# A fused attention and gated feed-forward block: side work moved to other places beside the matmul stream, with another DMA order and other buffer counts

## The chip, the core and the metric

The kernel runs on one core of a Trainium2 chip. The metric is the device time of one execution in microseconds (us); the median of three runs before the change is 272.18 us (271.14 to 272.46). The engines are named as the profile names them: PE (TensorE matmuls), PEld (its weight loads), DVE (VectorE), ACT (ScalarE), POOL (GpSimd) and SP (SyncE, which issues every DMA of this kernel). Each engine works through its own instructions in the order in which the program was written; between engines there are semaphores.

## What is computed

```python
x = A_x                                  # 1 x 2048 x 512, bf16
xn = layernorm(x)
qkv = xn @ wqkv                          # 512 x 1536; 32 heads of 16
# each position attends to 8 positions: itself and 2, 4, ... 14 positions back
logits = einsum("bhsd,bhswd->bhsw", q, kg) * 16 ** -0.5    # masked where idx < 0
o = einsum("bhsw,bhswd->bhsd", softmax(logits), vg)
s = o.reshape(B, S, D) @ wo              # 512 x 512
h = gelu(xn @ w_gate) * (xn @ w_up)      # 512 x 1792, twice
g = silu(h @ w_down)                     # 1792 x 512
return x + s * g
```

## The kernel before, in words

The 2048 positions are cut into four blocks of 512 (index j), and each block into four tiles of 128 (index t over all 16). Nothing reorders the program: the schedule is manual, so the order of the Python calls is the order on each engine. Per block, PE runs three long stages, and they are the frame for everything else:

- `qkv(j, 0..11)`: twelve groups of four 128x512 matmuls. Four give `q_sb`, four give `k_sb`, and four give V, which ACT copies into a staging tile `vst` and SP stores to `vT` in DRAM (L216).
- `glu(j, 0..13)`: fourteen pairs of four matmuls (`g_ps`, `u_ps`), ACT makes `ge` (Gelu) and `u`, DVE multiplies them into `h`.
- `down(j, 0..3)`: for each tile fourteen matmuls `y_ps` and four `s_ps`; ACT makes `sl` (Silu), DVE computes `m` and `o_t`, and SP stores `o_t` (L357).

Stages run as qkv 0, glu 0, qkv 1, down 0, glu 1, qkv 2, down 1, glu 2, qkv 3, down 2, glu 3, down 3. Beside them stands the side work:

- The layer norm of tile t: `moments(t)` (DVE `stats`, `mv`, then two POOL instructions for `rstd`), `normalize(t)` (DVE `xn`) and a transpose on PE (four small matmuls into the one PSUM tile `tr`, L179), copied by ACT into `xnT`.
- The window attention of block j: eight products `pk` (DVE, L235, 128x2048 each), summed over the head dimension on PE by `logits(j, 0)` and `logits(j, 1)` (`L_ps`), exponentiated on ACT (`E`), summed by `denominators` (`den_ps`, DVE reciprocal `rs`), spread over partitions (`sp_ps`, ACT `rb`), multiplied with V in eight products `pv` (DVE, L293) and summed on PE by `av_sum` (`o_ps`, then DVE `oT`). `pk` and `pv` share eight slots (`prod`), and `L_ps`, `den_ps`, `sp_ps` and `o_ps` share two PSUM banks (`att`).
- `load_v(j)` reads the shifted V windows back from `vT`, in four DMAs of 520 KB (L222). It needs all four `vst` stores of its block.

In the kernel before, `normalize(t)` transposes at once. Tiles 4 to 7 are normalized within qkv 0; tiles 8 to 11 have their moments ahead of, and their normalization behind, each tile of down 0; tiles 12 to 15 have both within qkv 2. `load_v(j + 1)` stands in one piece ahead of down j. `vst` has 3 buffers and `o_t` 2. SP issues x, wqkv, the gate and up weights, then w_down (`wd`), the rest of x and wo, and only then the small DMA of zeros into `vT` (`zpad`) and the first `vst` stores.

Of the kernel before, what the change touches and what calls it, by code (L numbers as in the profile page):

```python
# [28 lines left out]
def kernel(  # L29
# [23 lines left out]
    def pool(name, bufs, **kw):  # L53
        return ctx.enter_context(tc.tile_pool(name=name, bufs=bufs, **kw))
# [40 lines left out]
    for i in range(3):  # L95
        load_w(wqkv_sb, A_wqkv, i * D, (i + 1) * D)
    load_x(TPQ, TPQ)
    for lo, hi in ((0, DF // 2), (DF // 2, DF)):
        load_w(wg_sb, B_w_gate, lo, hi)
        load_w(wu_sb, B_w_up, lo, hi)  # L100
    nc.sync.dma_start(out=wd_sb[:], in_=B_w_down.rearrange("(k p) n -> p k n", p=P))
    load_x(2 * TPQ, TPQ)
    load_x(3 * TPQ, TPQ)
    for g in range(NC):
        nc.sync.dma_start(  # L105
            out=wo_sb[:, g, :],
            in_=bass.AP(tensor=A_wo.tensor, offset=g * 4 * D, ap=[[D, 4], [DH * D, H], [1, D]]),
        )


    ident = const.tile([P, P], BF16, name="ident")
# [21 lines left out]
        band(dsum[:, c, 8 * c : 8 * c + 8], 0, 16, 16, 1, 8)  # L133

    hsum = const.tile([P, H], BF16, name="hsum")
    for j in range(WL):
        nc.vector.tensor_copy(
            out=hsum[H * j : H * (j + 1), :], in_=ident[H * j : H * (j + 1), H * j : H * (j + 1)]
        )

    spread = const.tile([P, 4, P], BF16, name="spread")
    nc.vector.memset(spread[:], 0.0)
    for q in range(4):
        for j in range(4):
            nc.vector.tensor_copy(
                out=spread[H * q : H * (q + 1), q, H * j : H * (j + 1)],
                in_=ident[H * q : H * (q + 1), H * q : H * (q + 1)],
            )

    xnT = {}  # L150
    k_sb = big.tile([P, NC, PAD + S], BF16, name="k_sb")
# [8 lines left out]
    def moments(t):  # L160
# [4 lines left out]
        )  # L165
        nc.gpsimd.tensor_tensor(out=rstd[:, t, :], in0=rstd[:, t, :], in1=mhalf[:], op=ALU.pow)

    def normalize(t):
        xn = sm2.tile([P, D], BF16, name="xn")
        nc.vector.tensor_scalar(  # L170
            out=xn[:], in0=x_sb[:, t, :], scalar1=mv[:, t, 0:1], scalar2=rstd[:, t, :],
            op0=ALU.subtract, op1=ALU.mult,
        )
        transpose(t, xn)

    def transpose(t, xn):
        tr = trp.tile([P, NC * P], BF16, name="tr")
        for c in range(NC):
            nc.tensor.transpose(tr[:, c * P : (c + 1) * P], xn[:, c * P : (c + 1) * P], ident[:])  # L179
# [21 lines left out]
    def qkv(j, fo):  # L201
# [5 lines left out]
        if which == 0:  # L207
            nc.scalar.activation(out=st[j]["q"][:, c, :], in_=ps[:], func=AF.Copy)  # L208
        elif which == 1:
            lo = PAD + j * TQ  # L210
            nc.scalar.activation(out=k_sb[:, c, lo : lo + TQ], in_=ps[:], func=AF.Copy)  # L211
        else:
            vst = sm.tile([P, TQ], BF16, name="vst")
            nc.scalar.activation(out=vst[:], in_=ps[:], func=AF.Copy)  # L214
            lo = PAD + j * TQ
            nc.sync.dma_start(out=vT[c * P : (c + 1) * P, lo : lo + TQ], in_=vst[:])  # L216

    def load_v(j):

        va = vap.tile([P, DH, VW], BF16, name="v_arr")  # L220
        for wl in range(WL):
            nc.sync.dma_start(  # L222
                out=va[H * wl : H * (wl + 1), :, :],
                in_=bass.AP(
# [2 lines left out]
                    ap=[[SV * DH, H], [SV, DH], [1, VW]],  # L227
                ),
            )
        st[j]["va"] = va  # L230

    def qk_product(j, w):
        pk = prod.tile([P, NC, TQ], BF16, name="pk", tag="prod")
# [97 lines left out]
    def down(j, tt):  # L331
# [24 lines left out]
        nc.vector.tensor_tensor(out=o_t[:], in0=m[:], in1=x_sb[:, t, :], op=ALU.add)  # L356
        nc.sync.dma_start(out=out2d[t * P : (t + 1) * P, :], in_=o_t[:])  # L357


    for t in range(TPQ):  # L360
        moments(t)
        if t:
            normalize(t - 1)
    normalize(TPQ - 1)
    for t in range(TPQ, 2 * TPQ):
        moments(t)
    for fo in range(3 * NC):
        qkv(0, fo)
        if fo in (2, 4, 6, 8):
            normalize(TPQ + fo // 2 - 1)  # L370
    load_v(0)
    for j in range(NJ):
        for fc in range(NF):
            if j == 0:
                if fc < W:
                    qk_product(j, fc)
                if fc == 5:
                    logits(j, 0)
                if fc == 9:
                    logits(j, 1)  # L380
# [48 lines left out]

# [1 line left out]
_INS = ['A_x', 'A_wqkv', 'A_wo', 'B_x', 'B_w_gate', 'B_w_up', 'B_w_down']  # L431
_OUTS = [((1, 2048, 512), 'bfloat16')]
# [25 lines left out]
```

## Time and profile before

| What | us |
|---|---|
| Median of three runs | 272.18 |
| The profiled execution, its own time | 271.04 |
| Its span, first to last instruction | 269.3 |
| PE busy | 235.2 |
| DVE busy | 148.3 |
| ACT busy | 146.8 |
| POOL busy | 16.2 |

PE is busy for 87% of the span, and the next engine for 55%. The chain that ended last is PE for 71% of the span. The profiled execution's time is 1.74 us above its span. A window of the trace is given as its start and end in us from the span's start; in it, the busy time of an engine is followed by its count of instructions.

### The profile page before, as it was taken

What the parts mean: (1) busy time and instruction counts of PE and PEld (TensorE: products, weight loads), DVE (VectorE), ACT (ScalarE), POOL (GpSimd) and SP (SyncE); (2) the same over time, 40 slices, a digit from 0 to 9 for tenths busy, and PEclk for the clock granted to TensorE, in tenths of its full rate; (3) what the DMA queues carried; (4) which work ended last, traced back from release to release, by engine and by line L of the source; (5) the groups of instructions that cost most, each with busy time, mean ns of one, the idle gap of its engine ahead of it and who ended that gap; (6) DMA issues with size and microseconds to landing.
All of it is one profiled execution on the core that took longest, in us unless ns stands there. A gap on an engine that the chain in (4) does not pass through costs nothing.

```text
span 269.3 us, 3429 instructions
## 1 busy us (share of the span) xinstructions
PE 235.2 (87%) x1296; PEld 100.3 (37%) x1296; DVE 148.3 (55%) x242; ACT 146.8 (55%) x226; POOL 16.2 (6%) x60
## 2 busy tenths in 40 slices
PE   0599149999996769999899989999999959999993
PEld 0354013444332324434344434334444414334441
DVE  7631019537877671985454764893036454893231
ACT  1375057996551618665675638656773337656410
POOL 5430000000011110000130000000000000000000
PEclk9999858999999999999999999999999979999999
DMA  6999619600029700000004950000025920000001
GB/s 195 364 380 351 194 44 210 104 4 0 0 79 209 149 19 19 2 0 0 2 19 128 199 111 19 0 2 0 0 80 115 200 80 3 0 0 1 8 33 39
DMA packets 21793, 22.66 MB, mean 84 GB/s; under 512 B 1552, under 2 KB 21776, under 8 KB 21776
## 3 DMA queue, kind: packets, MB, share of 16 engines
q1 hardware_dynamic: 21776, 22.43, 32.6%
q8 instruction: 10, 0.16, 0.3%
q14 instruction: 7, 0.06, 0.1%
HBM read 18.22 MB, written 4.21 MB: 83 GB/s over the span
## 4 chain that ended last, share of the span: by engine, by line
PE 71%; SPq 11%; DMA 9%; DVE 6%; issue 1%; ACT 0%; POOL 0%; DVEq 0%; ACTq 0%
PE g_ps L191 19%; PE u_ps L191 18%; PE y_ps L334 12%; PE qkv_ps L191 11%; DMA out_dram<-o_t 7%; SPq L83 4%; PE s_ps L345 4%; PE o_ps L305 3%; PE L_ps L244 3%; SPq L89 3%; SPq L105 2%; DMA vT<-vst 2%; DVE m L354 2%; DVE pk L235 2%; DVE o_t L356 1%
## 5 line engine op out<-in xcount | busy, mean ns | idle before, releaser
L191 PE MATMUL g_ps<-xnT,wg_sb 128*128 128x512 bf16 x224 | 59.7, 390 | 9.0 <-ACT vst L214 9.0
L191 PE MATMUL u_ps<-xnT,wu_sb 128*128 128x512 bf16 x224 | 58.3, 383 | 0.0
L328 DVE TENSOR_TENSOR h<-ge,u 128x512 bf16<-128x512 bf16 x56 | 23.7, 423 | 59.7 <-ACT u L326 59.6
L334 PE MATMUL y_ps<-wd_sb,h 128*128 128x512 bf16 x224 | 51.0, 379 | 0.0
L191 PE MATMUL qkv_ps<-xnT,wqkv_sb 128*128 128x512 bf16 x192 | 45.2, 387 | 0.7 <-ACT xnT L183 0.7
L235 DVE TENSOR_TENSOR pk<-q_sb,k_sb 128x2048 bf16<-128x2048 bf16 x32 | 38.0, 1219 | 9.4 <-ACT k_sb L211 9.4
L324 ACT ACTIVATE ge<-g_ps 128x512 bf16<-128x512 f32 x56 | 33.6, 599 | 16.7 <-PE g_ps L191 16.6
L326 ACT ACTIVATE u<-u_ps 128x512 bf16<-128x512 f32 x56 | 33.5, 598 | 14.0 <-PE u_ps L191 14.0
L293 DVE TENSOR_TENSOR pv<-E,v_arr 128x2048 bf16<-128x2048 bf16 x32 | 38.6, 1217 | 0.0
L191 PEld LDWEIGHTS <-wg_sb 128*128 128x128 bf16 x224 | 20.5, 100 | 39.0 <-issue 19.1
L191 PEld LDWEIGHTS <-wu_sb 128*128 128x128 bf16 x224 | 22.1, 99 | 27.5 <-issue 1.8
L334 PEld LDWEIGHTS <-h 128*128 128x128 bf16 x224 | 21.5, 98 | 26.3 <-issue 1.3
L342 ACT ACTIVATE sl<-y_ps 128x512 bf16<-128x512 f32 x16 | 9.6, 597 | 33.2 <-PE y_ps L334 33.2
L354 DVE TENSOR_TENSOR m<-s_ps,sl 128x512 bf16<-128x512 f32 x16 | 11.1, 691 | 29.7 <-PE s_ps L345 29.7
L191 PEld LDWEIGHTS <-wqkv_sb 128*128 128x128 bf16 x192 | 18.5, 100 | 22.8 <-issue 3.8
L179 PE MATMUL tr<-ident,xn 128*128 128x128 bf16 x64 | 7.0, 240 | 16.2 <-DVE xn L170 14.2
L214 ACT ACTIVATE vst<-qkv_ps 128x512 bf16<-128x512 f32 x16 | 9.6, 597 | 17.4 <-DMA vT<-vst 12.0
L183 ACT ACTIVATE xnT<-tr 128x512 bf16<-128x512 bf16 x16 | 9.5, 595 | 17.2 <-PE tr L179 17.2
L345 PE MATMUL s_ps<-wo_sb,oT 128*128 128x512 bf16 x64 | 16.4, 379 | 0.0
L244 PE MATMUL L_ps<-pk,dsum 128*32 128x512 bf16 x128 | 10.9, 406 | 4.0 <-DVE pk L235 4.0
L208 ACT ACTIVATE q_sb<-qkv_ps 128x512 bf16<-128x512 f32 x16 | 9.6, 597 | 6.6 <-PE qkv_ps L191 6.6
L179 PEld LDWEIGHTS <-xn 128*128 128x128 bf16 x64 | 4.9, 105 | 20.8 <-DVE xn L170 18.7
(40 smaller groups left out, 133.0 us busy)
## 6 DMA issues: line engine op xcount, KB each, us to landing
v_arr<-vT SPq DMA_DIRECT2D x16, 520.0 KB, 10.2
vT<-vst SPq DMA_DIRECT2D x16, 128.0 KB, 1.7
out_dram<-o_t SPq DMA_DIRECT2D x16, 128.0 KB, 3.5
wg_sb<-in_B_w_gate_dram SPq DMA_DIRECT2D x2, 896.0 KB
wu_sb<-in_B_w_up_dram SPq DMA_DIRECT2D x2, 896.0 KB, 12.3
wd_sb<-in_B_w_down_dram SPq DMA_DIRECT2D x1, 1792.0 KB, 16.7
wqkv_sb<-in_A_wqkv_dram SPq DMA_DIRECT2D x3, 512.0 KB, 5.3
x_sb<-in_A_x_dram SPq DMA_DIRECT2D x3, 512.0 KB, 13.4
```

The source lines that it names most:

```text
L83: nc.sync.dma_start(out=x_sb[:, t : t + n, :], in_=x2d[t * P : (t + n) * P, :].rearrange("(t p) d -> p t d", p=P),)
L179: nc.tensor.transpose(tr[:, c * P : (c + 1) * P], xn[:, c * P : (c + 1) * P], ident[:])
L191: nc.tensor.matmul(ps[:], lhsT=w[:, dk, lo : lo + P], rhs=xnT[j][:, dk, :], start=(dk == 0), stop=(dk == NC - 1),)
L235: nc.vector.tensor_tensor(out=pk[:], in0=st[j]["q"][:], in1=k_sb[:, :, off : off + TQ], op=ALU.mult)
L244: nc.tensor.matmul(L[H * wl : H * (wl + 1), :], lhsT=dsum[:, c, :], rhs=st[j]["pk"][WL * wh + wl][:, c, :], start=(c == 0), stop=(c == NC ...
L293: nc.vector.tensor_tensor(out=pv[:], in0=st[j]["E"][:, wh, :].unsqueeze(1).to_broadcast([P, 4, TQ]), in1=st[j]["va"][:, 4 * g : 4 * g + 4, ...
L324: nc.scalar.activation(out=ge[:], in_=g_ps[:], func=AF.Gelu_apprx_tanh)
L326: nc.scalar.activation(out=u[:], in_=u_ps[:], func=AF.Copy)
L328: nc.vector.tensor_tensor(out=h[:], in0=ge[:], in1=u[:], op=ALU.mult)
L334: nc.tensor.matmul(y[:], lhsT=st[j][fc][:, tt * P : (tt + 1) * P], rhs=wd_sb[:, fc, :], start=(fc == 0), stop=(fc == NF - 1),)
L345: nc.tensor.matmul(s[:], lhsT=st[j]["oT"][:, g, tt * P : (tt + 1) * P], rhs=wo_sb[:, g, :], start=(g == 0), stop=(g == NC - 1),)
L354: nc.vector.tensor_tensor(out=m[:], in0=s[:], in1=sl[:], op=ALU.mult)
```

## The change

The calls of the side work move into a table (`at`), keyed by stage, block and position, and `run` calls what the table holds ahead of each PE group. The mathematics, the tiles and the instructions' shapes are as they were. The parts are:

1. DMA order on SP: the last two pieces of x go behind each half of the gate and up weights; `wd` and `wo` are issued after qkv 0 and `load_v(0)`.
2. `vst`, `o_t` and `xn` come from a pool of 4 buffers (3, 2 and 2 before); `q_sb`, `rb` and `oT` have 1 buffer (2 before).
3. The copies that build `hsum` and `spread` on DVE move from the program's start behind the normalization of the first four tiles.
4. `normalize` no longer transposes. The moments of tiles 8 to 11 go into qkv 0, their normalization into glu 0, their transposes into qkv 1; the moments of tiles 12 to 15 go into glu 0, their normalization and transposes into qkv 2.
5. Block 0's attention: `logits(0, 0)` at glu position 6 (5 before), `logits(0, 1)` at 10 (9), `denominators` at 12 (11), the spread and six `pv` products in qkv 1; each `av_sum` one position later there, its products apart from it.
6. Blocks 1 to 3: `logits(j, 0)` ahead of the last tile of down j-1 (the third before), `logits(j, 1)` at glu position 1 (0), `denominators` at 2 (1), the spread at 4 (3), each `av_sum` at 6, 8, 10, 12 (5, 7, 9, 11); three of the eight `pk` products of blocks 2 and 3 at the end of their qkv stage.
7. `load_v(j)` for j of 1 to 3 is cut into its four DMAs, one ahead of each tile of down j-1.

```diff
-    qp = pool("qp", 2)
+    qp = pool("qp", 1)
-    op = pool("op", 2)
+    op = pool("op", 1)
+    sm4 = pool("sm4", 4)
...
-    for lo, hi in ((0, DF // 2), (DF // 2, DF)):
+    for i, (lo, hi) in enumerate(((0, DF // 2), (DF // 2, DF))):
         load_w(wg_sb, B_w_gate, lo, hi)
         load_w(wu_sb, B_w_up, lo, hi)
-    nc.sync.dma_start(out=wd_sb[:], in_=B_w_down.rearrange("(k p) n -> p k n", p=P))
-    load_x(2 * TPQ, TPQ)
-    load_x(3 * TPQ, TPQ)
-    for g in range(NC):
-        nc.sync.dma_start(
-            out=wo_sb[:, g, :],
...
+        load_x((2 + i) * TPQ, TPQ)
+
+    def load_late_weights():
+        nc.sync.dma_start(out=wd_sb[:], in_=B_w_down.rearrange("(k p) n -> p k n", p=P))
...
     def normalize(t):
-        xn = sm2.tile([P, D], BF16, name="xn")
+        xn = xns[t] = sm4.tile([P, D], BF16, name="xn")
...
-        transpose(t, xn)
...
-            vst = sm.tile([P, TQ], BF16, name="vst")
+            vst = sm4.tile([P, TQ], BF16, name="vst")
...
-        o_t = sm2.tile([P, D], BF16, name="o_t")
+        o_t = sm4.tile([P, D], BF16, name="o_t")
...
+    for i in range(TPQ):
+        at(("qkv", 0, 1 + 2 * i), normalize, TPQ + i)
+        at(("qkv", 0, 3 + 2 * i), transpose, TPQ + i)
+        at(("qkv", 0, 8 + i), moments, 2 * TPQ + i)
+        at(("glu", 0, 8 + i), normalize, 2 * TPQ + i)
+        at(("qkv", 1, 1 + 3 * i), transpose, 2 * TPQ + i)
+        at(("glu", 0, 8 + i), moments, 3 * TPQ + i)
+        at(("qkv", 2, 2 * i), normalize, 3 * TPQ + i)
+        at(("qkv", 2, 3 + 2 * i), transpose, 3 * TPQ + i)
...
+    at(("glu", 0, 6), logits, 0, 0)
+    at(("glu", 0, 10), logits, 0, 1)
+    at(("glu", 0, 12), denominators, 0)
...
+    for j in range(1, NJ):
+        for w in range(W):
+            early = j > 1 and w < 3
+            at(("qkv", j, 9 + w) if early else ("down", j - 1, w // 2), qk_product, j, w)
+        for i in range(TPQ):
+            at(("down", j - 1, i), load_v, j, [i])
+        at(("down", j - 1, 3), logits, j, 0)
+        at(("glu", j, 1), logits, j, 1)
...
+    sum_constants()
...
     for fo in range(3 * NC):
+        run("qkv", 0, fo)
         qkv(0, fo)
-        if fo in (2, 4, 6, 8):
-            normalize(TPQ + fo // 2 - 1)
     load_v(0)
+    load_late_weights()
```

The order on SP at the program's start. A `DMAHW` number in brackets is one of eight completion counters that SP's DMAs take in turn: an instruction with it waits for an earlier DMA, at the start of the program for the one that was issued eight places before. Before, from `wd` on:

```order
L101 DMA wd_sb_108<-in_B_w_down_dram 128x14x512 [waits DMAHW4_49]
L83 DMA x_sb_104<-in_A_x_dram 128x4x512 [waits DMAHW5_49]
L83 DMA x_sb_104<-in_A_x_dram 128x4x512 [waits DMAHW6_49]
L105 DMA wo_sb_109<-in_A_wo_dram 128x1x512 [waits DMAHW7_49]
L105 DMA wo_sb_109<-in_A_wo_dram 128x1x512 [waits DMAHW0_49]
L105 DMA wo_sb_109<-in_A_wo_dram 128x1x512 [waits DMAHW1_49]
L105 DMA wo_sb_109<-in_A_wo_dram 128x1x512 [waits DMAHW2_49]
L115 DMA vT_110<-zpad_135 128x4x16 [waits DMAHW3_49,Pool_49]
L216 DMA vT_110<-vst_326 128x512 [waits DMAHW4_49,Activation_49]
L216 DMA vT_110<-vst_342 128x512 [waits DMAHW5_49,Activation_49]
```

And now, from the last piece of the gate weights on:

```order
L90 DMA wg_sb_109<-in_B_w_gate_dram 128x4x896 [waits DMAHW3_49]
L90 DMA wu_sb_110<-in_B_w_up_dram 128x4x896 [waits DMAHW4_49]
L84 DMA x_sb_107<-in_A_x_dram 128x4x512 [waits DMAHW5_49]
L119 DMA vT_113<-zpad_133 128x4x16 [waits DMAHW6_49,Pool_49]
L224 DMA vT_113<-vst_330 128x512 [waits DMAHW7_49,Activation_49]
L224 DMA vT_113<-vst_348 128x512 [waits DMAHW0_49,Activation_49]
L224 DMA vT_113<-vst_360 128x512 [waits DMAHW1_49,Activation_49]
L224 DMA vT_113<-vst_372 128x512 [waits DMAHW2_49,Activation_49]
L232 DMA v_arr_375<-vT_113 32x16x520 [waits DMAHW3_49,DMAHW6_49,DMAHW2_49,DMAHW7_49,DMAHW1_49,DMAHW0_49]
L232 DMA v_arr_375<-vT_113 32x16x520 [waits DMAHW4_49]
L232 DMA v_arr_375<-vT_113 32x16x520 [waits DMAHW5_49]
L105 DMA wd_sb_111<-in_B_w_down_dram 128x14x512
```

The zeros and the `vst` stores stand ahead of `wd` and `wo`; the first store's counter is now that of the second piece of x and no longer that of `wd`, which comes behind the V windows.

The order on DVE in the first two tiles of down 0 (`pk` of block 1, `stats`, `mv` and `xn` of tiles 8 and 9, `m` and `o_t` of tiles 0 and 1). Before:

```order
L235 TENSOR_TENSOR pk_811<-q_sb_672,k_sb_175 128x2048 [waits DVE_49,Activation_49]
L235 TENSOR_TENSOR pk_813<-q_sb_672,k_sb_175 128x2048 [waits DVE_49]
L161 BN_STATS stats_177<-x_sb_104 128x6 [waits DMAHW5_49]
L162 BN_AGGR mv_178<-stats_177 128x2 [waits DVE_49]
L354 TENSOR_TENSOR m_841<-s_ps_836,sl_834 128x512 [waits PE_49,Activation_49]
L356 TENSOR_TENSOR o_t_843<-m_841,x_sb_104 128x512 [waits DVE_49]
L170 TENSOR_SCALAR xn_846<-x_sb_104,mv_178,rstd_181 128x512 [waits Pool_49]
L235 TENSOR_TENSOR pk_855<-q_sb_672,k_sb_175 128x2048
L235 TENSOR_TENSOR pk_857<-q_sb_672,k_sb_175 128x2048
```

Now:

```order
L244 TENSOR_TENSOR pk_874<-q_sb_715,k_sb_152 128x2048 [waits DVE_49,Activation_49]
L244 TENSOR_TENSOR pk_876<-q_sb_715,k_sb_152 128x2048 [waits DVE_49]
L363 TENSOR_TENSOR m_902<-s_ps_897,sl_895 128x512 [waits PE_49,Activation_49]
L365 TENSOR_TENSOR o_t_904<-m_902,x_sb_107 128x512 [waits DVE_49]
L244 TENSOR_TENSOR pk_907<-q_sb_715,k_sb_152 128x2048
L244 TENSOR_TENSOR pk_909<-q_sb_715,k_sb_152 128x2048
L363 TENSOR_TENSOR m_934<-s_ps_929,sl_927 128x512 [waits PE_49,Activation_49]
```

The moments and `xn` are gone from between the tiles; with them goes, on PE, the transpose that stood between two tiles and waited for `xn`, which itself stood behind `m` and `o_t`.

The order on SP in down 0. Before, the four V windows in one piece, then the stores of the four output tiles:

```order
L222 DMA v_arr_806<-vT_110 32x16x520 x3
L357 DMA out_0_dram<-o_t_843 128x512 [waits DVE_49]
L357 DMA out_0_dram<-o_t_887 128x512 [waits DVE_49]
L357 DMA out_0_dram<-o_t_949 128x512 [waits DVE_49]
L357 DMA out_0_dram<-o_t_992 128x512 [waits DVE_49]
```

Now:

```order
L366 DMA out_0_dram<-o_t_904 128x512 [waits DMAHW1_49,DVE_49]
L232 DMA v_arr_878<-vT_113 32x16x520 [waits DMAHW2_49]
L366 DMA out_0_dram<-o_t_936 128x512 [waits DMAHW3_49,DVE_49]
L232 DMA v_arr_878<-vT_113 32x16x520
L366 DMA out_0_dram<-o_t_968 128x512 [waits DVE_49]
L232 DMA v_arr_878<-vT_113 32x16x520
L366 DMA out_0_dram<-o_t_1019 128x512 [waits DVE_49]
```

Windows and stores alternate, so that a window's DMA stands behind a store that waits for its output tile.

More of the change, by code (lines that the diff above doesn't have):

```diff
@@ L173, in normalize, with transpose @@
         )
-        transpose(t, xn)
-    def transpose(t, xn):
+    def transpose(t):
+        xn = xns[t]
         tr = trp.tile([P, NC * P], BF16, name="tr")
@@ L216, in qkv, with load_v @@
             nc.sync.dma_start(out=vT[c * P : (c + 1) * P, lo : lo + TQ], in_=vst[:])
-    def load_v(j):
-        va = vap.tile([P, DH, VW], BF16, name="v_arr")
-        for wl in range(WL):
+    def load_v(j, wls=range(WL)):
+        if wls[0] == 0:
+            st[j]["va"] = vap.tile([P, DH, VW], BF16, name="v_arr")
+        va = st[j]["va"]
+        for wl in wls:
             nc.sync.dma_start(
@@ L229, in load_v @@
             )
-        st[j]["va"] = va
     def qk_product(j, w):
@@ L363 @@
             normalize(t - 1)
+            transpose(t - 1)
     normalize(TPQ - 1)
+    transpose(TPQ - 1)
+    sum_constants()
     for t in range(TPQ, 2 * TPQ):
```

102 lines of the change are left out of this document (42 added, 60 removed).

## The prediction

> **What bounds the kernel now.** First the stages: the windows cut at the first matmul of each stage show how long PE needed and how much of it was idle (in order: glu 0, qkv 1, down 0, glu 1, qkv 2, down 1, glu 2, qkv 3, down 2, glu 3, down 3 with the tail; the lead-in takes the 24.4 us ahead of them).
>
> ```profile
> core 0: us, PE busy (x) PEld busy (x) DVE busy (x) ACT busy (x) POOL busy (x), PEclk, DMA share, GB/s
> 24.40:63.10 38.70, 29.66 (x157) 12.36 (x156) 14.54 (x22) 23.43 (x36) 0.68 (x7) 0.87 0.50 119
> 63.10:76.70 13.60, 13.50 (x81) 5.12 (x80) 11.58 (x14) 7.16 (x12) 0.00 (x0) 1.00 0.06 20
> 76.70:102.60 25.90, 19.33 (x122) 8.28 (x121) 17.95 (x28) 10.10 (x14) 3.15 (x8) 1.00 0.54 113
> 102.60:129.90 27.30, 27.30 (x160) 11.37 (x157) 17.64 (x26) 19.06 (x31) 0.00 (x0) 1.00 0.00 1
> 129.90:142.20 12.30, 11.45 (x65) 5.49 (x64) 7.26 (x15) 8.74 (x15) 3.15 (x8) 1.00 0.05 18
> 142.20:161.80 19.60, 18.46 (x109) 7.76 (x106) 11.46 (x15) 9.20 (x11) 0.00 (x0) 1.00 0.70 146
> 161.80:189.20 27.40, 27.40 (x158) 11.43 (x158) 17.91 (x27) 18.38 (x30) 0.00 (x0) 1.00 0.02 5
> 189.20:199.50 10.30, 10.30 (x50) 4.62 (x49) 2.79 (x3) 7.17 (x12) 0.00 (x0) 1.00 0.04 15
> 199.50:221.60 22.10, 19.23 (x105) 7.85 (x103) 11.19 (x14) 8.71 (x10) 0.00 (x0) 0.95 0.62 132
> 221.60:249.50 27.90, 27.90 (x157) 11.50 (x157) 17.88 (x26) 18.38 (x30) 0.00 (x0) 0.98 0.02 6
> 249.50:269.30 19.80, 15.72 (x73) 6.92 (x71) 4.89 (x9) 4.27 (x6) 0.00 (x0) 1.00 0.08 27
> ```
>
> PE sets the pace: in glu 1, glu 2, qkv 3 and glu 3 it has no idle time, while DVE and ACT reach two thirds. The idle time sits in few stages: 9.0 us in glu 0 (38.7 less 29.66), 6.6 in down 0, 0.85 in qkv 2, 1.1 in down 1, 2.9 in down 2. The list of waits names them:
>
> ```profile
> PE tr L179 <- DVE xn L170: 14.2, 6, 6.8
> PE g_ps L191 <- ACT vst L214: 9.0, 1, 9.0
> DVE o_t L356 <- DMA out_dram<-o_t: 6.0, 2, 3.9
> PE L_ps L244 <- DVE pk L235: 4.0, 4, 2.1
> ```
>
> Of the 14.2 us, 6.8 are the first transpose of the program; the other 7.4 are down 0 and qkv 2. Then the timeline of the longest wait, SP's queue beside ACT:
>
> ```profile
> 28.79 1.36 SPq L115 DMA_DIRECT2D vT<-zpad  x1
> 30.25 7.07 SPq L216 DMA_DIRECT2D vT<-vst  x4
> 36.38 0.60 ACT L214 ACTIVATE vst<-qkv_ps 128x512 bf16<-128x512 f32 x1 [12.03 <-DMA vT<-vst]
> ```
>
> The fourth `vst` needs the slot of the first, whose store left SP only at 30.25 because the weights stood ahead of it; behind that ACT instruction wait all later PSUM evictions, so PE stopped.
>
> **What a stage costs when nothing stops it.** From the chain of waits and PE's timeline:
>
> ```profile
> 88.74 0.98 PE L_ps L244 x16
> 165.75 0.86 PE g_ps L191 x4
> 166.61 0.86 PE u_ps L191 x4
> 199.66 3.02 PE y_ps L334 x14
> 202.68 0.86 PE s_ps L345 x4
> ```
>
> ```profile
> 17.70 0.39 PE L179 MATMUL tr<-ident,xn 128*128 128x128 bf16 x4
> 17.92 1.89 PE L191 MATMUL qkv_ps<-xnT,wqkv_sb 128*128 128x512 bf16 x8
> ```
>
> A glu pair is 1.72, fourteen are 24.1. glu 2 took 27.4 with denominators, spread and four sums, so these side groups cost 3.3; the denominators are 0.4 of it (0.30 in a row below, and 0.1 for the switch), which leaves 2.9 for spread and sums. `logits` is 0.98 + 0.1 = 1.1. A transpose in a running stream is 0.22 (17.70 to 17.92). qkv is 10.3, a tile of down 3.88, four 15.5.
>
> **The change part by part.** (1) The start. `zpad` and the `vst` stores no longer stand behind `wd` and `wo`, and the fourth `vst` has a slot of its own. That takes out the 9.0 us, and the slow matmuls behind it (granted clock in the second window 0.87 over the stage). glu 0 becomes 24.1 + 2 × 1.1 + 0.4 = 26.7 instead of 38.7: **-12.0**. What is late next? The second halves of the weights, needed at glu position 7, 24.4 + 12.1 + 1.1 = 37.6 us. Before, `zpad` waited for the second `wu` half and left at 28.79, so it had landed by then; now one piece of x (512 KB) lies ahead of it, at most a quarter of the 10.2 us that four windows took in the row below: 31.4 at the latest. The V windows need the stores: the last `vst` ends near 25.3 (qkv 0's end and ACT's 0.60), a store took at most 6.1 (30.25 to 36.38), the windows 10.2; they land by 42 and are used at 50.
>
> ```profile
> v_arr<-vT SPq DMA_DIRECT2D x16, 520.0 KB, 10.2
> wd_sb<-in_B_w_down_dram SPq DMA_DIRECT2D x1, 1792.0 KB, 16.7
> ```
>
> `wd` issues behind them at 34 at the latest and lands 16.7 us later, at 51; down 0 begins at 65. The copies on DVE stood ahead of the first moments:
>
> ```profile
> 2.56 1.65 DVE L145 COPY spread<-ident 32x32 bf16<-32x32 bf16 x16
> ```
>
> They end at 4.2 and may have held the first moments up by about a microsecond, which comes back if x has landed; but now they delay the moments of tile 4, whose transpose PE wants after three qkv groups. I take +0.2 for the lead-in, between -0.9 (all comes back) and +1.65 (all is paid again).
>
> (2) Layer norms. down 0 loses its four transposes with their 6.6 us of waiting, and one `logits` to glu 1: 15.5 + 1.1 = 16.6 instead of 25.9: **-9.3**. qkv 1 gains four transposes (0.9) and the spread, but its sums now stand a group behind their products, which end in time: 10.3 + 2.9 + 0.9 = 14.1 against 13.6: **+0.5**. qkv 2 has its moments done: 10.3 + 0.9 = 11.2 against 12.3: **-1.1**.
>
> (3) V traffic, `o_t` and the early products. In down 1 and down 2 DVE stood at `o_t` for 2.1 and 3.9 us, because two buffers waited for stores queued behind 2 MB of windows; the last `pk` came late, then the second `logits`, then PE. With four buffers a tile waits for a store one whole block old. Each becomes 16.6: **-3.0** and **-5.5**. The `logits` that leave the down stages put 1.1 on glu 1, 2 and 3: 28.5 each, against 27.3, 27.4 and 27.9 (the last began at a low clock): **+2.9**. The last window now leaves SP behind the third `o_t`, some 7 us ahead of the next stage's products; 520 KB are a quarter of what took 10.2.
>
> Sum: -12.0 - 9.3 + 0.5 - 1.1 - 3.0 - 5.5 + 2.9 + 0.2 = **-27.3**, a span of 242.0 if no new wait appears.
>
> **New waits.** In blocks 1 to 3 `E` of the second half now follows `ge` and `u` of the first pair, with one more pair of table loads than before.
>
> ```profile
> 103.62 0.60 ACT L254 ACTIVATE E<-L_ps 128x512 bf16<-128x512 f32 x1
> 104.23 1.28 ACT L324 ACT_TABLE_LOAD   x1
> 104.41 0.30 PE L267 MATMUL den_ps<-E,hsum 128*32 128x128 bf16 x8
> 105.53 0.60 ACT L324 ACTIVATE ge<-g_ps 128x512 bf16<-128x512 f32 x1
> ```
>
> From the start of glu 1 on ACT: the Gelu table until 1.0, `ge` 1.7, `u` (done on PE at 1.7) 2.7, the Exp table 3.9, `E` 4.5; PE arrives at the denominators at 1.7 + 1.1 + 1.7 = 4.5. Then `rs` stands behind the second `h`: Gelu table 5.8, `ge` and `u` 7.0, `h` 7.5, `rs` 8.4; PE reaches the spread at 8.4. Both are level: I take 0.25 per block, 0.75 in all; bounds 0 and one `rs`, 1 us each. [...]
>
> DVE in glu 0 is the other candidate:
>
> ```profile
> L235 DVE TENSOR_TENSOR pk<-q_sb,k_sb 128x2048 bf16<-128x2048 bf16 x32 | 38.0, 1219 | 9.4 <-ACT k_sb L211 9.4
> L328 DVE TENSOR_TENSOR h<-ge,u 128x512 bf16<-128x512 bf16 x56 | 23.7, 423 | 59.7 <-ACT u L326 59.6
> L161 DVE BATCH_NORM_STATS2 stats<-x_sb 128x6 f32<-128x512 bf16 x16 | 10.9, 681 | 1.3 <-DMA x_sb<-in_A_x_dram 1.3
> L162 DVE BATCH_NORM_AGGREGATE mv<-stats 128x2 f32<-128x6 f32 x16 | 2.9, 182 | 0.6
> L170 DVE TENSOR_SCALAR xn<-x_sb,mv,rstd 128x512 bf16<-128x512 bf16 x16 | 6.4, 408 | 7.3 <-POOL rstd L166 5.0 <-PE tr L179 2.4
> L276 DVE RECIPROCAL rs<-den_ps 128x128 bf16<-128x128 f32 x4 | 3.8, 950 | 0.0
> L166 POOL TENSOR_TENSOR rstd<-rstd,mhalf 128x1 f32<-128x1 f32 x16 | 9.2, 574 | 1.3
> ```
>
> Eight `pk` 9.8, fourteen `h` 5.9, four moments 3.5, four `xn` 1.6, `rs` 0.95, two `pv` (as `pk`) 2.4: 24.1 us of work in a stage of 26.7, begun some 3 us late with the first `h` (one `pk` is done ahead). So `rs` ends at about 50.8 and PE wants it at 51; the first sum wants its `pv` at 53.4 and has it at 53.6. I take 0.5, between 0 and 3. With 0.75 that is 1.2: span 243.2, time 243.2 + 1.74 = 245.0 beside the profiled 271.04. The median shown is 1.0042 of that execution; so **246 us**.
>
> **Rivals.** (a) DVE becomes the bound in block 0. For it: the thin slack. Against: in down 0, 17.95 of 25.9 us were busy. [...]
>
> [...]
>
> (c) The V traffic still delays `o_t` or `pv`, since each window on SP now waits behind a store. If the stalls of down 1 and 2 came back, that is 8.5 us less the two `logits` (2.2) that only moved: 6.3, so 252. Against: four buffers.
>
> (d) The change doesn't do what it says at the start: a store or weight is late and the 12.0 us stay: 258.
>
> (e) Slower: the granted clock. Unbroken stretches now are at most the 55 us from 161.8 to 216, at 1.00 in the windows; afterwards PE runs unbroken from 24 to 238. If the clock fell in the 160 us beyond the first 55, the price is 160 × (1/c - 1), and the kernel is slower once that passes 26 us, at c below 0.86; at 0.84 it would be 276. Against it: the only low clocks stand at the stalls.
>
> **How the numbers follow.** The forecast has 0.74, its own range 243 to 249 (the lead-in 0.9 earlier and no new wait, to 3 us more of either); (a) 0.12, (b) 0.03, (c) 0.06, (d) 0.02, (e) 0.03. The range of 243 to 251.5 takes in (a) and the edge of (c). A measurement here tells 0.5% (1.4 us) from no change; all cases but (e) are faster by more: 0.96 faster, 0.01 same, 0.03 slower.
>
> **What would show it.** Right: no wait of PE on `vst`, `xn` after 12 us, or `pk`; glu 0 near 27, each down near 16.6, DVE no longer waiting at `o_t`; PE idle only in the lead-in and the tail. Wrong: PE waiting for `rs` or `pv` in qkv 1 (a), for `E` at the denominators (b), DVE at `o_t` or `pv` on a DMA (c), PE on weights (d), a granted clock below 0.95 in a stage without stalls (e).

## The result, and the profile after

The changed kernel takes **243.05 us** (median of four runs, 242.86 to 243.32) against 272.32 for the kernel before (271.14 to 272.56, now with a fourth run): a ratio of 0.893, 95% interval 0.891 to 0.896. The forecast was 246.0. Its profiled execution took 243.32, with a span of 241.6 and so 1.72 around it.

The head of the page of the kernel after: busy time by engine, PE and its granted clock in 40 slices, and the shares of the chain that ended last:

```profile
PE 228.0 (94%) x1271; PEld 99.4 (41%) x1296; DVE 145.8 (60%) x242; ACT 149.4 (62%) x229; POOL 17.3 (7%) x60
...
PE   1599999999999999999999999999999999999993
...
PEclk9999999999999999999999999999999999999999
...
PE 94%; POOL 1%; ACT 1%; issue 1%; DVE 1%; POOLq 0%; DVEq 0%
```

PE now stands still only at the start and at the end. The windows of the kernel after, cut at the first matmul of each stage, with the columns that the prediction's windows have (lead-in, glu 0, qkv 1, down 0, glu 1, qkv 2, down 1, glu 2, qkv 3, down 2, glu 3, down 3 with the tail):

```profile
0.00:24.30 24.30, 16.12 (x79) 7.97 (x81) 16.12 (x55) 12.19 (x20) 13.33 (x45) 1.00 0.94 309
24.30:51.00 26.70, 26.54 (x151) 11.52 (x153) 18.14 (x33) 23.11 (x35) 3.92 (x15) 1.00 0.78 184
51.00:65.10 14.10, 13.99 (x100) 5.98 (x101) 11.88 (x15) 9.55 (x17) 0.00 (x0) 1.00 0.05 19
65.10:81.70 16.60, 16.50 (x88) 7.27 (x89) 12.34 (x14) 7.49 (x10) 0.00 (x0) 1.00 0.67 160
81.70:110.10 28.40, 28.24 (x170) 11.61 (x172) 18.40 (x28) 20.51 (x32) 0.00 (x0) 1.00 0.05 11
110.10:121.40 11.30, 11.25 (x65) 5.63 (x65) 4.60 (x8) 9.12 (x16) 0.00 (x0) 1.00 0.04 14
121.40:138.00 16.60, 16.39 (x88) 7.27 (x89) 9.64 (x12) 7.38 (x9) 0.00 (x0) 1.00 0.61 150
138.00:166.40 28.40, 28.24 (x170) 11.60 (x172) 18.40 (x28) 20.57 (x33) 0.00 (x0) 1.00 0.08 21
166.40:176.80 10.40, 10.35 (x49) 4.73 (x49) 3.08 (x4) 7.17 (x12) 0.00 (x0) 1.00 0.04 16
176.80:193.40 16.60, 16.50 (x88) 7.25 (x89) 9.87 (x12) 7.49 (x10) 0.00 (x0) 1.00 0.71 167
193.40:221.80 28.40, 28.24 (x170) 11.62 (x172) 18.40 (x28) 20.51 (x32) 0.00 (x0) 1.00 0.04 10
221.80:241.60 19.80, 15.61 (x71) 6.94 (x71) 4.89 (x9) 4.27 (x6) 0.00 (x0) 0.99 0.08 27
```

Every stage is within 0.3 us of its term: glu 0 26.7 (26.7 predicted), qkv 1 14.1 (14.1), each down 16.6 (16.6), the later glu 28.4 (28.5), qkv 2 11.3 (11.2), the lead-in 24.3 (24.6). Of the waits that PE has left, in the list of waits of the kernel after, all but 0.2 us lie ahead of the first qkv group. The two longest:

```profile
PE tr L187 <- DVE xn L178: 5.4, 1, 5.4
...
PE tr L187 <- ACT xnT L191: 2.1, 3, 0.7
```

From the first matmul of glu 0 to the first of down 3 the kernel before took 225.1 us. That stretch of the kernel after, as one window:

```profile
24.31:221.81 197.50, 196.24 (x1124) 84.48 (x1144) 124.76 (x178) 132.90 (x203) 3.92 (x15) 1.00 0.31 74
```

The same window of an experiment below, the one with two `o_t` buffers:

```profile
24.70:222.20 197.50, 197.50 (x1146) 84.46 (x1144) 124.75 (x178) 132.88 (x203) 3.91 (x15) 1.00 0.31 74
```

And of the last experiment below, the one with another start:

```profile
21.66:219.16 197.50, 197.50 (x1145) 84.46 (x1144) 126.40 (x181) 132.88 (x203) 6.17 (x20) 1.00 0.32 77
```

It is 197.50 in each, to the hundredth: PE is its only bound there. So this stretch, in each kernel's profiled execution, is a sharper measure than the time of a run; below it is called the stretch.

### The profile page after: what moved, and what is told of

Its sections match the earlier page's. It is cut to its first block, busy times and chain, and to the rows that moved or that the text cites. A ratio compares the mean times of both kernels' runs of the same rounds, so it can differ in the third digit from the quotient of the medians.

```text
span 241.6 us, 3413 instructions
## 1 busy us (share of the span) xinstructions
PE 228.0 (94%) x1271; PEld 99.4 (41%) x1296; DVE 145.8 (60%) x242; ACT 149.4 (62%) x229; POOL 17.3 (7%) x60
## 4 chain that ended last, share of the span: by engine, by line
PE 94%; POOL 1%; ACT 1%; issue 1%; DVE 1%; POOLq 0%; DVEq 0%
PE g_ps L199 21%; PE y_ps L343 20%; PE u_ps L199 19%; PE qkv_ps L199 18%; PE s_ps L354 6%; PE o_ps L314 4%; PE L_ps L253 3%; PE tr L187 2%; ACT xnT L191 1%; PE den_ps L276 0%; PE sp_ps L291 0%; POOL dsum L123 0%; POOL dsum L127 0%; DVE m L363 0%; ACT E L263 0%
## 5 line engine op out<-in xcount | busy, mean ns | idle before, releaser
L199 PE MATMUL g_ps<-xnT,wg_sb 128*128 128x512 bf16 x217 | 57.2, 380 | 0.5
L199 PE MATMUL u_ps<-xnT,wu_sb 128*128 128x512 bf16 x219 | 56.6, 379 | 0.1
L343 PE MATMUL y_ps<-wd_sb,h 128*128 128x512 bf16 x217 | 50.4, 379 | 0.5 <-issue 0.2
L199 PE MATMUL qkv_ps<-xnT,wqkv_sb 128*128 128x512 bf16 x187 | 47.0, 395 | 0.9 <-ACT xnT L191 0.7
L343 PEld LDWEIGHTS <-h 128*128 128x128 bf16 x224 | 21.6, 98 | 27.0 <-issue 1.3
L199 PEld LDWEIGHTS <-wg_sb 128*128 128x128 bf16 x224 | 20.1, 98 | 28.4 <-issue 7.2
L167 DVE BATCH_NORM_STATS2 stats<-x_sb 128x6 f32<-128x512 bf16 x16 | 10.8, 677 | 3.2 <-DMA x_sb<-in_A_x_dram 3.1
L323 DVE TENSOR_TENSOR oT<-o_ps,rb 128x512 bf16<-128x512 f32 x16 | 11.0, 685 | 2.2 <-PE o_ps L314 2.2
```

Source lines behind the costliest of these rows:

```text
L199: nc.tensor.matmul(ps[:], lhsT=w[:, dk, lo : lo + P], rhs=xnT[j][:, dk, :], start=(dk == 0), stop=(dk == NC - 1),)
L323: nc.vector.tensor_tensor(out=st[j]["oT"][:, g, :], in0=o[:], in1=st[j]["rb"][:], op=ALU.mult)
L343: nc.tensor.matmul(y[:], lhsT=st[j][fc][:, tt * P : (tt + 1) * P], rhs=wd_sb[:, fc, :], start=(fc == 0), stop=(fc == NF - 1),)
```

## The experiments

### Parts of the change put on the kernel before

**A fourth `vst` buffer alone.**

```diff
+    vsp = pool("vsp", 4)
-            vst = sm.tile([P, TQ], BF16, name="vst")
+            vst = vsp.tile([P, TQ], BF16, name="vst")
```

> The kernel before with one edit: vst has 4 buffers of its own instead of 3. Theory A (the slot alone is the cause of PE's 9.0 us): ACT's fourth vst no longer waits, PE runs through, glu 0 falls from 38.7 to about 27 and the time to 260.4 us, although the stores still leave SP only at 30; the V windows then land at about 47 and are used at 50. Theory B (the DMA order is what matters): the late stores hold something else, the V windows or down 0, and less than 4 us is won (268 or more).

Measured: 260.55 us (259.06 to 261.20), ratio 0.955 (0.949 to 0.960). SP and ACT in this kernel's timeline:

```profile
24.57 0.60 ACT L215 ACTIVATE vst<-qkv_ps 128x512 bf16<-128x512 f32 x1 [0.27 <-PE qkv_ps L192]
...
30.38 2.71 SPq L217 DMA_DIRECT2D vT<-vst  x4
```

The stores leave as late as before, at 30.38, but the fourth copy has its slot and ACT goes on at 24.57. glu 0 falls from 38.7 to 27.1. The late store cost time only through the missing buffer, and it cost more than the 9.0 us of waiting: the stage is 11.6 shorter.

**The new DMA order alone**, with three `vst` buffers.

```diff
-    for lo, hi in ((0, DF // 2), (DF // 2, DF)):
+    for i, (lo, hi) in enumerate(((0, DF // 2), (DF // 2, DF))):
         load_w(wg_sb, B_w_gate, lo, hi)
         load_w(wu_sb, B_w_up, lo, hi)
-    nc.sync.dma_start(out=wd_sb[:], ...)   # and x, x, wo
+        load_x((2 + i) * TPQ, TPQ)
+    def load_late_weights(): ...           # wd, wo
     load_v(0)
+    load_late_weights()
```

> The kernel before with the new DMA order alone (zeros and stores ahead of wd and wo, x between the weights), vst still with 3 buffers. Theory A' (either edit is enough): the first store lands 2 us after it is issued at 22.4, before the fourth vst wants its slot at 24.5, and the time is 260.4 us, as with the buffers alone. Theory B' (the slot is needed too): the first store takes the 6 us that it took before, ACT waits until 28.5, PE stops for 1 to 2 us: 262 or more.

Measured: 262.34 us (260.77 to 263.45), ratio 0.962 (0.957 to 0.967). ACT still waits once, but little:

```profile
25.46 0.60 ACT L214 ACTIVATE vst<-qkv_ps 128x512 bf16<-128x512 f32 x1 [0.74 <-DMA vT<-vst]
```

That is the profiled execution, the 260.77, where PE loses nothing by it: glu 0 is 27.1. The median lies where the second theory had it; the three others have no trace, so what they lost stays open. Order and buffer each give 10 to 12 us, and the two take out one and the same wait (glu 0 is 27.1 with either, and 26.9 in the kernel after, which has both): their gains don't add.

**The layer norms alone** (part 4 for tiles 8 to 15, `xn` with four buffers, `q_sb` with one).

```diff
+        if fo >= 8:
+            moments(2 * TPQ + fo - 8)
         qkv(0, fo)
...
+                if 8 <= fc < 12:
+                    normalize(fc, False)
+                    moments(TPQ + fc)
...
+                if i % 3 == 1:
+                    transpose(2 * TPQ + i // 3)
                 qkv(1, i)
...
-            if j == 0:
-                moments(2 * TPQ + tt)
             down(j, tt)
-            if j == 0:
-                normalize(2 * TPQ + tt)
```

> The kernel before with the layer norms of tiles 8 to 15 at the places of the change (and q_sb with 1 buffer, for space). Theory: down 0 loses 6.6 us of waiting, four transposes (0.9) and the slow restarts, qkv 1 gains four transposes, qkv 2 loses 1.1: 8.3 us in all, 264.0. Rival (DVE in glu 0 and qkv 1 is filled by it and the attention of block 0 comes late): 4 us or less, 268 or more.

Measured: 267.80 us (265.97 to 268.98), ratio 0.982 (0.975 to 0.988), 4 us less than hoped. In this kernel's list of waits DVE stands at x:

```profile
DVE stats L162 <- DMA x_sb<-in_A_x_dram: 13.7, 2, 12.2
```

PE stands behind it in the lead-in, in the timeline of the same kernel:

```profile
29.45 0.61 PE L184 MATMUL tr<-ident,xn 128*128 128x128 bf16 x4 [6.87 <-DVE xn L173]
```

The moments of tile 8 now stand on DVE ahead of the `xn` of tile 7, and in the old order their x comes behind `wd`. The lead-in grows from 24.4 to 34.1; ACT's wait for a `vst` slot falls from 12.0 to 3.0 with the fourth `vst` some 10 us later, not by any edit to the buffer. Part 4 needs part 1.

**Order and norms together.** The two edits above.

> The kernel before with the new DMA order and the moved layer norms together (vst 3 buffers, q_sb 1). Theory: in the run with the norms alone DVE stood 12 us at the moments of tile 8, whose x came behind wd; with x ahead of the second weights that wait goes, and the norms bring their whole term of 8.3 us on top of the order's 262.3: 254.0. Rival: the norms are worth no more than they brought alone (4.7 us) because DVE is full in glu 0: 257.6.

Measured: 259.70 us (258.64 to 260.59), ratio 0.950 (0.944 to 0.957). Both expectations missed: the norms, worth 9.9 in the prediction (8.8 without the `logits` that only moves), take 2.6 off the median of the order alone, and 0.4 off the stretch. Down 0 in this kernel's timeline:

```profile
84.27 0.43 DVE L361 TENSOR_TENSOR o_t<-m,x_sb 128x512 bf16<-128x512 bf16 x1 [3.37 <-DMA out_dram<-o_t]
...
87.02 1.86 PE L249 MATMUL L_ps<-pk,dsum 128*32 128x512 bf16 x13 [0.76 <-DVE pk L240]
```

With the `xn` waits gone, the four tiles of down 0 come so close together that its third `o_t` runs into a store that is still queued behind the V windows. Before, the `xn` waits kept the tiles 6 to 7 us apart and hid this; it is the same stall as in down 1 and 2. PE waits for `pk` seven times in this kernel, 8.3 us in all, against 4 times and 4.0 before. By stage, read from PE's timeline of each kernel (us from a stage's first matmul to the next one's; a transpose or spread ahead of that counts to the stage before, so some numbers differ by 0.2 from the windows):

| Kernel | lead-in | glu 0 | down 0 | down 1 | down 2 | glu 1, 2, 3 | glu 0 to down 3 |
|---|---|---|---|---|---|---|---|
| before | 24.4 | 38.7 | 25.8 | 19.6 | 22.2 | 27.4, 27.3, 27.9 | 225.1 |
| `vst` buffer | 24.4 | 27.1 | 25.8 | 20.1 | 22.6 | 27.3, 27.3, 28.0 | 214.6 |
| order | 24.8 | 27.1 | 25.8 | 19.9 | 22.2 | 27.3, 27.3, 28.6 | 214.5 |
| norms | 34.1 | 29.4 | 20.6 | 21.3 | 21.2 | 29.0, 29.0, 27.4 | 213.4 |
| order and norms | 24.6 | 28.8 | 21.6 | 22.2 | 21.5 | 27.9, 27.9, 28.7 | 214.1 |
| after | 24.3 | 26.9 | 16.6 | 16.6 | 16.6 | 28.4, 28.4, 28.4 | 197.5 |

The other 16.6 us of the stretch come only when the buffers, the attention's new places and the cut windows (parts 2, 5, 6 and 7) join in; what each of these brings by itself was not run. In the run with order and norms 9.3 of the 16.6 are idle time of PE: 1.2 in glu 0, where it waits 0.6 for `rs`, and 2.3, 2.9 and 2.8 in down 0, 1 and 2. In the other 7.4 PE counts as busy but needs longer for the same matmuls. The thirteen `L_ps` matmuls behind the wait at 87.02 take 1.86, thirteen behind a wait of 0.22 at 34.40 take 1.02. The granted clock is 0.7 in three of the 40 slices of this run's page (84 to 90, 149 to 155 and 207 to 213 us, at the ends of down 0, 1 and 2), against 0.9 or more in all 40 of the kernel after; so a stall cost more here than its wait.

### Parts taken out of the kernel after

**Two `o_t` buffers and V windows in one piece.**

```diff
-        o_t = sm4.tile([P, D], BF16, name="o_t")
+        o_t = sm2.tile([P, D], BF16, name="o_t")
...
-        for i in range(TPQ):
-            at(("down", j - 1, i), load_v, j, [i])
+        at(("down", j - 1, 0), load_v, j)
```

> The changed kernel with the V windows in one piece again and o_t with 2 buffers again; all else stays. Theory C (the o_t wait comes back but the later logits and the early products now cover most of it): DVE waits 2 to 4 us at o_t in down 1 and down 2, PE stops for 1 us at most in each: 243.1 to 245. Theory D (these two edits carry the whole of that term): 6.3 us come back, 249.4.

Measured: 246.84 us (246.18 to 247.13), 3.8 above the kernel after and between the two expectations. The old wait is back, here in this kernel's timeline: DVE stands at `o_t` for 13.0 us in all, against 6.0 before. PE loses less by it: each down is still 16.6, and glu 1, 2 and 3 take 29.2, 28.9 and 30.9, since the `logits` that need the late `pk` now stand later.

```profile
137.84 0.42 DVE L365 TENSOR_TENSOR o_t<-m,x_sb 128x512 bf16<-128x512 bf16 x1 [3.59 <-DMA out_dram<-o_t]
```

**Two `o_t` buffers alone**, the first of these two edits.

> The changed kernel with o_t in 2 buffers again, V windows still cut in four. Theory E (the cut alone keeps the queue short: stores land within 2 to 4 us, a tile takes 3.9): no wait at o_t, 243.0 to 243.4. Theory F (the buffers are what removed the wait): the 3.8 us of the run with both undone come back, 246.8.

Measured: 243.39 us (243.04 to 243.71).

**V windows in one piece alone**, the second edit.

> The changed kernel with the V windows in one piece again, o_t in 4 buffers. Theory E' (either edit is enough): no wait at o_t, since the slot's store is a block old, 243.0 to 243.4. Theory F' (the cut is what removed it): 246.8.

Measured: 243.17 us (242.87 to 243.34). The DMA view of the kernel after, with the median time from issue to landing of the output stores:

```profile
out_dram<-o_t SPq DMA_DIRECT2D x16, 128.0 KB, 1.9
```

The same row here:

```profile
out_dram<-o_t SPq DMA_DIRECT2D x16, 128.0 KB, 6.3
```

The stores are three times as late behind whole windows, and nobody waits with four buffers. Either part of the change is enough by itself; with one of them undone the stretch is 197.50, and both undone cost 3.7 us of it (201.22).

**The copies of the constants back at the program's start.**

```diff
+    sum_constants()
     for t in range(TPQ):
         moments(t)
...
     transpose(TPQ - 1)
-    sum_constants()
```

> The changed kernel with the hsum and spread copies at the program's start again. Theory G (the first qkv groups run at half clock until a point that does not move with their start): the first transpose comes 1.4 us later, at 6.75, but glu 0 begins within 0.3 us of 24.3, and the time is 242.8 to 243.4. Rival (the lead-in is set by DVE's start): glu 0 begins at 25.7, 244.4.

Measured: 244.23 us (243.16 to 244.69, six runs), which decides nothing. The median is near the rival's 244.4, and five of the six runs lie above every run of the kernel after. The sixth is the profiled execution, the 243.16, and bears the first theory out: the first qkv group starts 1.23 us later than in the kernel after, at 11.72, but its twelve matmuls take only 3.92, and the lead-in is 24.15, no longer than there. The stretch is 197.50 here too. Of the other runs there is no trace, so where their time went stays open.

### Costs added to the kernel after

**Two more DVE products** in glu 0 (their results are not read).

```diff
+        nc.vector.tensor_tensor(out=sp[:], in0=st[0]["q"][:], in1=k_sb[:, :, PAD : PAD + TQ], op=ALU.mult)
+    for i in range(2):
+        at(("glu", 0, 11), spare_product)
```

> The changed kernel with two extra products of the size of pk on DVE at position 11 of glu 0, 2.44 us, never read. Theory (the slack ahead of the spread is what the trace shows, rs done at 50.60 and PE there at 50.98, 0.4 us): PE waits 2.0 us for rs, and perhaps a few tenths at the first sum: 245.1. Rival (DVE has room that the trace hides): 243.0 to 243.6.

Measured: 245.27 us (245.13 to 245.97). The added work took 2.45 us, and 2.13 of them show in the stretch (199.63):

```profile
48.99 2.45 DVE L398 TENSOR_TENSOR spare<-q_sb,k_sb 128x2048 bf16<-128x2048 bf16 x2
...
52.70 0.38 PE L292 MATMUL sp_ps<-rs,spread 128*128 128x128 bf16 x4 [1.90 <-DVE rs L286]
```

**One more ACT copy** ahead of the second `E` in blocks 1 to 3 (not read either).

```diff
+        nc.scalar.activation(out=sc[:], in_=x_sb[:, 0, :], func=AF.Copy)
+        at(("glu", j, 1), spare_copy)
```

> The changed kernel with one extra ACT copy of 128x512 (0.6 us, never read) ahead of the second half's E in blocks 1 to 3. Theory (the slack at the denominators is 0.2 us: E done at 86.13, PE there at 86.32): PE waits 0.4 us in each of three blocks, 1.3 us in all, 244.3. Rival (no slack is used up, because PE's queue of groups covers it): 243.0 to 243.3.

Measured: 244.40 us (244.12 to 244.67); the stretch is 198.70, 0.40 more in each of three blocks for a copy of 0.6. Here the denominators last until `E` comes, 0.61 us against 0.29:

```profile
85.64 0.60 ACT L264 ACTIVATE E<-L_ps 128x512 bf16<-128x512 f32 x1
85.92 0.61 PE L277 MATMUL den_ps<-E,hsum 128*32 128x128 bf16 x8
```

Both show that the kernel after stands close to the next bound on both sides: some 0.3 us of room on DVE in block 0, 0.2 on ACT in the others.

**Seven more POOL products**, each released by an `h` so that it may fall on a `pk` (not read; one run).

```diff
+        nc.gpsimd.tensor_tensor(out=pt[:, i : i + 1], in0=st[0][i - 1][:, 0:1], in1=mhalf[:], op=ALU.mult)
+    for i in range(1, W):
+        at(("glu", 0, i), spare_pool, i)
```

> The changed kernel with seven extra POOL products of 128x1 with two inputs, each released by the h of one glu pair, so that it falls on the pk that DVE starts at the same moment; never read. [...] Rival Q: the pk are held by them, 1.8 us each, and glu 0 grows. Rival R: neither changes.

Measured: 243.06 us, stretch 197.50. Timeline of DVE and POOL:

```profile
27.60 1.22 DVE L244 TENSOR_TENSOR pk<-q_sb,k_sb 128x2048 bf16<-128x2048 bf16 x1
27.76 1.10 POOL L398 TENSOR_TENSOR pt<-h,mhalf 128x1 f32<-128x1 bf16 x1 [4.61 <-DVE h L337]
...
37.72 0.19 POOL L398 TENSOR_TENSOR pt<-h,mhalf 128x1 f32<-128x1 bf16 x1
```

Beside a `pk` the POOL instruction takes 1.10 us, until that `pk` ends, six times out of seven; the seventh came without one and takes 0.19. The `pk` stays at 1.22, against rival Q, and the POOL instruction doesn't, against rival R.

### A version that beats both

**PE kept busy from the start, and the transposes of tiles 4 to 7 later.** Matmuls on a constant tile, never read, fill PE's idle time ahead of and between the first transposes; tiles 4 to 7 are normalized right behind their moments and the copies of the constants come after that.

```diff
+    warm_ps = mm.tile([P, TQ], F32, name="warm_ps", tag="mm")
+    def warm(n):
+        for _ in range(n):
+            nc.tensor.matmul(warm_ps[:], lhsT=wsrc[:, 0:P], rhs=wsrc[:], start=True, stop=True)
...
+    warm(9)
     for t in range(TPQ):
...
             transpose(t - 1)
+            warm(2)
     normalize(TPQ - 1)
     transpose(TPQ - 1)
-    sum_constants()
+    warm(2)
...
+    for t in range(TPQ, 2 * TPQ):
+        normalize(t)
+    sum_constants()
...
-        at(("qkv", 0, 1 + 2 * i), normalize, TPQ + i)
-        at(("qkv", 0, 3 + 2 * i), transpose, TPQ + i)
+        at(("qkv", 0, 8 + i), transpose, TPQ + i)
```

> The changed kernel with extra matmuls on a constant tile while PE has nothing to do (nine ahead of the first transpose, two behind each of the first four), normalization of tiles 4 to 7 right behind their moments, the hsum and spread copies behind these, and the transposes of tiles 4 to 7 at qkv positions 8 to 11; the extra products are never read. Theory G (the lead-in kept its 24.3 us because the first twelve matmuls run at half clock, 5.28 us, however early they start): they now take 2.6 us, glu 0 begins at 21.7, 240.5. Rival H (the slow matmuls are not a matter of the clock, or the clock does not react to these): 243 or more.

Measured: **240.66 us** in each of four runs, ratio 0.881 (0.877 to 0.886) to the kernel before, and 2.4 below the kernel after. PE's start in the timeline of the kernel after:

```profile
10.49 5.28 PE L199 MATMUL qkv_ps<-xnT,wqkv_sb 128*128 128x512 bf16 x12 [0.69 <-ACT xnT L191]
15.56 0.47 PE L187 MATMUL tr<-ident,xn 128*128 128x128 bf16 x4
```

And here, with DVE's instructions for tiles 4 to 6:

```profile
1.55 3.55 PE L166 MATMUL warm_ps<-wsrc 128*128 128x512 bf16 x9 [1.55 <-DVE wsrc L161]
...
9.92 7.07 PE L208 MATMUL qkv_ps<-xnT,wqkv_sb 128*128 128x512 bf16 x32 [0.25 <-ACT xnT L200]
...
11.40 0.69 DVE L176 BATCH_NORM_STATS2 stats<-x_sb 128x6 f32<-128x512 bf16 x1 [2.62 <-DMA x_sb<-in_A_x_dram]
...
14.62 1.04 DVE L187 TENSOR_SCALAR xn<-x_sb,mv,rstd 128x512 bf16<-128x512 bf16 x3
...
16.82 0.39 PE L196 MATMUL tr<-ident,xn 128*128 128x128 bf16 x4
```

Twelve matmuls took 15.56 - 10.49 = 5.07 us in the kernel after, 0.42 each; here 32 took 6.90, 0.216 each. glu 0 begins at 21.66. The run has both edits in it; what each alone would do was not run and is an estimate from these rows. x for tile 4 lands at 11.4, and its `xn` is done near 15.0. Fast matmuls with the transposes in their old places would stop at 9.92 + 12 × 0.216 = 12.5, go on at 15.0 with 36 matmuls and four transposes of 0.22, and reach glu 0 at 23.7, 0.6 earlier than in the kernel after. Slow matmuls with later transposes would do 20 more matmuls from 15.56 to 19.9, then four transposes and 16 matmuls, and reach it at 24.2, 0.1 earlier. By this it takes the two together.

## Why the prediction was right, and where it missed

The direction, the place of every gain and the stage times were right. The time measured lies 2.95 us under the forecast, at the lower edge of the range given.

**The sum of the terms** gave a span of 242.0 and 241.6 came; the 0.4 are the lead-in (0.3), the later glu stages (0.1 each) and, the other way, qkv 2 and 3. That -12.0, -9.3, -3.0 and -5.5 add up so well is no proof of each: the experiments show that the parts don't add. The -12.0 is had in nearly the same size by the buffer or by the order (38.7 to 27.1 with either). The -9.3 isn't had by the norms: on top of the order, down 0 fell by 4.2 us, glu 0 rose by 1.7 and down 1 by 2.3. What the prediction's step (2) didn't see is a third `o_t` stall in down 0 that the `xn` waits had hidden; it called the stalls of step (3) a matter of down 1 and down 2. The whole came out because it priced the stages as they are with no wait left, 15.5 + 1.1, and the full change removes that third stall with the other two.

**The new waits** were the term that was mis-sized: 1.2 us predicted, 0 measured. Block 1 of the kernel after, ACT and DVE against PE:

```profile
85.53 0.60 ACT L263 ACTIVATE E<-L_ps 128x512 bf16<-128x512 f32 x1
86.14 1.28 ACT L333 ACT_TABLE_LOAD   x1
86.32 0.29 PE L276 MATMUL den_ps<-E,hsum 128*32 128x128 bf16 x8
87.44 0.60 ACT L333 ACTIVATE ge<-g_ps 128x512 bf16<-128x512 f32 x1
...
88.90 0.95 DVE L285 RECIPROCAL rs<-den_ps 128x128 bf16<-128x128 f32 x1
...
90.01 0.39 PE L291 MATMUL sp_ps<-rs,spread 128*128 128x128 bf16 x4
```

`E` ends at 86.13 and PE wants it at 86.32; `rs` ends at 89.85 and PE wants it at 90.01. "Both are level" was the right reading, to 0.2 us, but a race that is level by the sum can fall on either side, and 0.25 per block was a mean of the two. Block 0, where DVE was thought 0.5 late:

```profile
49.65 0.95 DVE L285 RECIPROCAL rs<-den_ps 128x128 bf16<-128x128 f32 x1
...
50.98 0.39 PE L291 MATMUL sp_ps<-rs,spread 128*128 128x128 bf16 x4
...
51.93 1.22 DVE L302 TENSOR_TENSOR pv<-E,v_arr 128x2048 bf16<-128x2048 bf16 x1
53.25 0.61 PE L314 MATMUL o_ps<-pv,hsum 128*32 128x512 bf16 x8
```

`rs` has 0.4 of room, and the first sum's `pv` 0.1. The predicted end of `rs`, 50.8, came as 50.6, but the way there was wrong: 24.1 us of DVE work were reckoned without a pause, and the window shows 18.1 busy: two products and two `h` fall outside the stage, neighbouring instructions overlap by some 0.1 us each, and DVE waited in between for ACT's `u`, 2.75 us ahead of the `h` at 39.87.

**The step from span to time.** 1.74 was 1.72. The factor 1.0042, the kernel before's median over its profiled execution, added 1.0 us and shouldn't have: the kernel after's median lies 0.27 below its profiled execution. One execution's place among its kernel's runs said nothing of the next kernel's.

**The lead-in** was put at 24.6, between 23.7 and 26.0, and came at 24.3; in the profiled executions of the seven kernels with the changed start it ran from 23.84 (two `o_t` buffers and whole windows) to 24.70 (two `o_t` buffers). The step had half of the mechanism. The copies did hold the first moments up (PE's first wait is 5.4 now and was 6.8), but of these 1.4 us only 0.1 came back. Three things can be the last ahead of the transpose of tile 4. In the kernel after it is the first twelve matmuls: they take 5.28 us instead of the 4.06 that PE's timeline of the kernel before has for them, and the transpose behind them waits for nothing. With two `o_t` buffers and whole windows DVE comes to tile 4 at the same time, 11.50, the same matmuls take 4.14, and the transpose waits for `xn`; the lead-in is 23.84. PE there:

```profile
10.47 4.14 PE L199 MATMUL qkv_ps<-xnT,wqkv_sb 128*128 128x512 bf16 x12 [0.69 <-ACT xnT L191]
15.17 0.40 PE L187 MATMUL tr<-ident,xn 128*128 128x128 bf16 x4 [0.56 <-DVE xn L178]
```

The other two are the copies and x, whichever ends later. DVE in the timeline of the kernel after:

```profile
9.82 1.64 DVE L151 COPY spread<-ident 32x32 bf16<-32x32 bf16 x16
11.49 0.69 DVE L167 BATCH_NORM_STATS2 stats<-x_sb 128x6 f32<-128x512 bf16 x1
```

And with two `o_t` buffers:

```profile
12.36 0.69 DVE L167 BATCH_NORM_STATS2 stats<-x_sb 128x6 f32<-128x512 bf16 x1 [0.93 <-DMA x_sb<-in_A_x_dram]
```

In the one the moments follow the copies at once; in the other they wait for x until 12.36, and the lead-in is 24.70. So the lead-in moves by most of a microsecond (23.84 to 24.70) with the time of the first matmuls (4.14 to 5.28) and the arrival of x (12.36, or by 11.49), which differ between these executions; the stretch is 197.50 in the kernel after and with two `o_t` buffers alike.

**The rivals.** (a) DVE as the bound of block 0: no, but 0.3 us from it, as the added products showed. The range went up to 251.5 to take it in with POOL holding DVE up, and no run shows that. In the POOL experiment it is POOL that is held: 1.10 us beside a `pk` against 0.19 without one, with the `pk` at 1.22 each time and the stretch at 197.50. In all six cases the `pk` had started first (27.60 against 27.76 in the rows above); a POOL instruction that starts first isn't in them. (b) No: PE doesn't wait for `E`, which ends at 86.13, 0.2 us ahead of it. `ge` starts 0.02 us after its table load ends (87.44 after 86.14 + 1.28), as in the kernel before (105.53 after 104.23 + 1.28); no run shows a change of tables that holds ACT for longer than its load. (c) No: DVE doesn't wait at `o_t`; with both covers taken away the price is 3.7, not 6.3, though DVE's wait is longer than before; the later `logits` hide the rest. (d) No: nothing waits for a `vst` slot or a weight, and glu 0 is 26.7. (e) No: the granted clock is 0.99 or 1.00 in every window, through 197.5 us without a pause.

## What to carry to other kernels

Price a stage by what its bound engine needs with no wait left, and check that every wait in it goes: take one of two waits away and the other, which it had hidden, takes its place, so the gains of parts don't add. Where two engines are level by a sum, the wait may be nothing at all: keep both ends in the range, and look which one the rows are nearer to; here the mean of the two was 1.2 us too much. The long stall here cost more than its wait: 9.0 us at `vst` were 11.6 of the stage. Where the middle of a program repeats to the hundredth, compare variants on that stretch, and look for the scatter at the program's start.

## What the runs showed of the hardware that had not been expected

At the start of the kernel after PE's matmuls take 0.42 us each until about 15.5 us and then 0.216, while the granted clock in the window of the lead-in reads 1.00; so that column doesn't show it, and the "half clock" of the expectations is the author's reading of what was measured as half the speed. In the six other kernels that start in the same way, the first twelve of these matmuls begin at 10.46 or 10.47 and take 4.14 to 4.99 us, so the step to 0.216 comes earlier there than in the kernel after. Matmuls ahead of the first transposes, with the later transposes of tiles 4 to 7, removed the slow start of the qkv groups, and with it 2.4 us and the scatter between runs (240.66 four times, against 242.86 to 243.32). In that kernel's trace the nine added matmuls from 1.55 on took 3.55 us together, with their weight loads 0.43 apart, and the 32 from 9.92 on take 0.216 each. In the kernel after the matmuls of 0.42 go on for 5.07 us from the first qkv group on. Why PE is slow at the start, and for longer in one execution than in another, no run here shows.
